# Own places in TensorE's order for scores, sums and values, by kind of segment, in a recurrent attention kernel with streamed weights

## The chip, the core and the metric

The kernel runs on one core of a Trainium2 chip. The metric is the device time of one launch in microseconds (us), the median over runs. Engines are named as in the profile: PE is TensorE's matmuls, PEld its weight loads, DVE is VectorE, ACT is ScalarE, POOL is GpSimd, SP is SyncE, which here only issues transfers (DMAs).

## The reference, cut to what matters

Two branches read the same layer-normed `x` (2048 rows of 1024) and are added to it: a dense branch with a GELU, and a recurrent attention.

```python
for s in range(n_seg):                       # 64 segments of 32 rows
    h = concatenate([mem, xs], axis=1)       # 8 memory rows and the segment's 32
    q, k, v = h @ Wq, h @ Wk, h @ Wv         # 1024 -> 32 heads of 128
    p = softmax(where(mask, q @ k.T * scale, -1e9))
    o = (p @ v) @ Wo                         # 4096 -> 1024
    mem = o[:, :M, :].copy()                 # the next segment's memory
    outs.append(o[:, M:, :])
```

A segment cannot begin before the one ahead of it has its 8 output memory rows. All four weight matrices are used in every segment, and they do not fit on the core together.

## The kernel before, in words

**Two stages.** The first (up to about 430 us) makes the dense branch for all rows and lays out, in DRAM, the transposed inputs and the residual rows of every segment. The second is the recurrence, 64 segments one after another, some 22 us each. The change touches the second alone.

**Weights.** Each of the four matrices is cut into 16 units of 128x2048 elements, 512 KB each. 46 of the 64 units stay on the core, 18 are `STREAMED` in each segment: 16 by a DMA from DRAM, 2 by a DVE copy out of PSUM (line 240). Six slots hold streamed units. When PE has used a streamed unit, `unit_done` (it is called after each unit) lets the slot go and starts the next transfer in the list on SP's queue (lines 251 and 253), so a transfer begins when PE releases a slot and has six streamed units of lead.

**The order within a segment.** PE's order is written out by hand. Six half passes of 8 units each come first, K0, Q0, K1, Q1, V0, V1 (the digit is the half of the heads, 16 heads each), and then 16 units of the output product, O. A unit of a half pass is four 128x512 products side by side, one per 32 columns of the array (line 705). `half_pass(w, u, left, at)` takes a dictionary `at` from a unit's number to pieces of work that stand in PE's order after that unit; the O loop has the same. These pieces are:

- `scores(u)`: 32 small products (lines 807 and 813) into the PSUM tile `mixed`, an exponential on ACT (819), two mask operations on DVE (826).
- `sums(u)`: 8 products that add up the exponentials (834, 840), then on ACT a logarithm and two exponentials (845, 848), then on DVE the two tiles of normalised weights, `pd_main` (855) and `pd_left` (859).
- `values(u, rs)`: for each of 4 columns of heads a main product with this segment's V (874) and a left product with V of the left rows (880). `rs` are the two row halves of the array; each half has its own PSUM bank and is copied out by ACT (half 0) or DVE (half 1), line 888.

**Left rows.** Only 24 of the 32 rows of a segment go with its own pass; the last 8 rows of the four segments of a group are done together, as extra products (`hL`, "left") on the same units. Which passes carry them depends on the place in the group, `i4 = s % 4`, so there are four kinds of segment. Kind 0 carries left products in K1 and V0, kind 1 in Q0 and in O (twice the length), kind 2 in Q1, kind 3 in K0 and V1. A unit with left products takes PE twice as long.

**The Q1 and V1 passes around the change.** The transposition of Q1 that `scores(1)` needs runs thus: `sums(0)` in the Q1 pass; on ACT the logarithm and exponentials of `sums(0)`, then the cast of Q1 (line 749, `b_oL`); on DVE `pd_main`, `pd_left`, and only then the transposition (763). Both engines work in the order of their instructions. PE meanwhile does the rest of Q1, the whole of V0, and the first unit of V1. In kind 0 the left rows of V0 are cast by DVE (753, tile `VL`) just ahead of `values(0)`. In kind 2 `keep_q(1)` copies queries into a part of `mixed` (line 240) between `scores(0)` and `sums(0)`. The results of `values(1)` are the inputs (`b_oL`) of O's units 8 to 15, those of `values(0)` (`d_oL`) of units 0 to 7. Three PSUM banks (`acc`) go round among the passes and the values.

Of the kernel before, what the change touches and what calls it, by code (L numbers as in the profile page):

```python
# [86 lines left out]
def kernel(  # L87
# [177 lines left out]
    def load_left_rows(g, eng=nc.sync):  # L265
        hr = hrp.tile([P, 256], BF16, name="hrL")
        eng.dma_start(out=hr[:, :], in_=hrL_d[g, :, 0:256])
        nxt["hL"] = hr.rearrange("p (k t) -> p k t", k=KT)
# [346 lines left out]
    with tc.tile_pool(name="late", bufs=1) as late, \  # L615
# [10 lines left out]
        def new_acc():  # L626
            bank = free_banks.popleft()
            ps = banks.tile([P, 512], F32, name="acc", tag=bank)
            bank_of[id(ps)] = bank, ps
            return ps  # L630

        def let_go(ps):
            free_banks.append(bank_of.pop(id(ps))[0])
# [47 lines left out]
        for s in range(NSEG):  # L681
            g, i4 = divmod(s, GRP)
# [96 lines left out]
            def q_left(u):  # L779

                if i4 >= 2 + u and more:
                    q = qS[:, i4 - 2 - u, :, :]
                else:
                    q = qL[u][:, :, NL * i4:NL * i4 + NL]
                nc.vector.tensor_copy(out=q_home[:, :, 0:NL], in_=q)

            def ends(t):

                return t.rearrange("p c (a b) -> p c a b", b=NL)[:, :, ::4, :]
# [9 lines left out]
            def scores(u, meanwhile=None):  # L799

                kT, qL_ends = st["kT", u], ends(q_home)
                sA = mixed[:, 0:160].rearrange("p (c q) -> p c q", q=40)
                sB = mixed[:, 160:224].rearrange("p (c q) -> p c q", q=16)
                for c in range(4):
                    for j in range(4):
                        q = slice(32 * j, 32 * j + 32)
                        nc.tensor.matmul(  # L807
                            sA[q, c, :], lhsT=kT[:, 4 * c + j, :], rhs=q_home[:, 4 * c + j, :],
                            start=(c == 0), stop=True, skip_group_check=True, tile_position=(0, 32 * j),
                        )  # L810
                    for j in range(4):
                        q = slice(32 * j, 32 * j + 32)
                        nc.tensor.matmul(
                            sB[q, c, :].rearrange("p (a b) -> p a b", b=NL), lhsT=kL[u][:, 4 * c + j, :],
                            rhs=qL_ends[:, 4 * c + j, :, :],
                            start=False, stop=True, skip_group_check=True, tile_position=(0, 32 * j),
                        )
                pr = pr_all[:, 0:224]
                nc.scalar.activation(out=pr, in_=mixed[:, 0:224], func=ACT.Exp, scale=INV_SQRT_DH)
                prA = pr[:, 0:160].rearrange("p (c q) -> p c q", q=40)  # L820
                prB = pr[:, 160:224].rearrange("p (c q) -> p c q", q=16)
                if meanwhile is not None:
                    meanwhile()
                for p, m in ((prA[:, :, NL:SEG], mask_order), (prB, mask_left[:, i4, :])):
                    n = m.shape[-1]
                    nc.vector.tensor_tensor(out=p, in0=p, in1=m[:, None, :].to_broadcast([P, 4, n]), op=ALU.min)
                st["pr", u] = prA, prB

            def sums(u):
                prA, prB = st["pr", u]  # L830
                dA = mixed[:, 0:160].rearrange("p (c q) -> p c q", q=40)
                for j in range(4):
                    q = slice(32 * j, 32 * j + 32)
                    nc.tensor.matmul(
                        dA[q, :, :], lhsT=bd[:, j:j + 1].to_broadcast([P, 32]), rhs=prA, start=True, stop=False,
                        skip_group_check=True, tile_position=(0, 32 * j),
                    )
                for j in range(4):
                    q = slice(32 * j, 32 * j + 32)
                    nc.tensor.matmul(  # L840
                        ends(dA[q, :, :]), lhsT=bd[:, j:j + 1].to_broadcast([P, 32]),
                        rhs=prB.rearrange("p c (a b) -> p c a b", b=NL),
                        start=False, stop=True, skip_group_check=True, tile_position=(0, 32 * j),
                    )
                nc.scalar.activation(out=mixed[:, 0:160], in_=mixed[:, 0:160], func=ACT.Ln)  # L845

                for b in (1, 0):
                    nc.scalar.activation(  # L848
                        out=mixed[:, 160 * b:160 * b + 160], in_=mixed[:, 0:160], func=ACT.Exp, scale=-1.0,
                        bias=off[:, b:b + 1],  # L850
                    )
                pdA = pd_main.rearrange("p (c b q) -> p c b q", c=4, b=2)
                pdB = pd_left.rearrange("p (c b a q) -> p c b a q", c=4, b=2, q=NL)
                dd = mixed[:, 0:320].rearrange("p (b c q) -> p b c q", b=2, q=40)
                nc.vector.tensor_tensor(  # L855
                    out=pdA.rearrange("p c b q -> p b c q"), in0=prA[:, None, :, :].to_broadcast([P, 2, 4, 40]),
                    in1=dd, op=ALU.mult,
                )
                nc.vector.tensor_tensor(
                    out=pdB.rearrange("p c b a q -> p b c a q"),  # L860
                    in0=prB.rearrange("p c (a q) -> p c a q", q=NL)[:, None, :, :, :].to_broadcast([P, 2, 4, 2, NL]),
                    in1=dd.rearrange("p b c (e q) -> p b c e q", q=NL)[:, :, :, ::4, :], op=ALU.mult,
                )
                st["pd", u] = pdA, pdB

            def values(u, rs):

                V, (pdA, pdB) = st["V", u], st["pd", u]
                av = {r: new_acc() for r in rs}
                oV = {r: av[r][:, 0:320].rearrange("p (c b q) -> p c b q", c=4, b=2) for r in rs}  # L870
                for c in range(4):
                    for r in rs:
                        q = slice(64 * r, 64 * r + 64)
                        nc.tensor.matmul(  # L874
                            oV[r][:, c, :, :], lhsT=V[q, c * P:(c + 1) * P], rhs=pdA[q, c, :, :],
                            start=(c == 0), stop=False, skip_group_check=True, tile_position=(64 * r, 0),
                        )
                    for r in rs:
                        q = slice(64 * r, 64 * r + 64)
                        nc.tensor.matmul(  # L880
                            oV[r].rearrange("p c b (e q) -> p c b e q", q=NL)[:, c, :, ::4, :],
                            lhsT=VL[u][q, c * P:(c + 1) * P], rhs=pdB[q, c, :, :, :],
                            start=False, stop=True, skip_group_check=True, tile_position=(64 * r, 0),
                        )
                for r in rs:
                    cp = nc.vector.tensor_copy if r else nc.scalar.copy
                    out = outs[u][:, 8 * r:8 * r + 8, NL * slot:NL * slot + 40]
                    cp(out=out.rearrange("p (b c) q -> p c b q", b=2), in_=oV[r])
                    let_go(av[r])
# [32 lines left out]
            at = {} if first else {1: [lambda: q_left(0)]}  # L922
# [7 lines left out]
            if left_q[0] and not first:  # L930
# [3 lines left out]
            rows_out(psK1, nat_home, nc.scalar.copy)  # L934
            at = {
                0: [lambda: scores(0, None if first else lambda: q_left(1)), lambda: nc.vector.transpose(out=nat_home, in_=nat_home)],
                6: [lambda: sums(0)],
            }
            if left_q[1] and not first:
                at[0].insert(1, lambda: keep_q(1))  # L940
# [14 lines left out]
                left_values(0, psVL)  # L955
            if i4 == 0 and more and not first:
                load_left_rows(g + 1, nc.scalar)
            at = {0: [lambda: scores(1)], 4: [lambda: sums(1)]}
            if left_v[1]:
                at.update({1: [lambda: values(0, (0,))], 3: [lambda: values(0, (1,))]})  # L960
            else:
                at[1] = [lambda: values(0, (0, 1))]

            def load_res():
                st["res"] = res_home
# [15 lines left out]
            if left_v[1]:  # L981
                at = {4: [lambda: values(1, (0,))], 6: [lambda: values(1, (1,))]}
            else:
                at = {5: [lambda: values(1, (0, 1))]}
            if left_v[1] and not first:
                at[9] = [lambda: left_values(1, psV1L)]
            at.setdefault(0, []).append(load_res)
# [42 lines left out]
            if final:  # L1030
                engines = [nc.sync, nc.scalar, nc.gpsimd]
                n = 0
# [57 lines left out]
```

The softmax here doesn't subtract the row's maximum and nothing guards it: scores larger than these inputs give would overflow.

## Time and profile before

| | us |
|---|---|
| median of three runs | 1876.3 |
| the runs | 1868.09, 1877.63, 1876.3 |
| span of the profiled execution, first to last instruction | 1866.2 |
| PE busy in it | 1726.3 |
| DVE, ACT, POOL busy | 904.3, 650.4, 257.7 |
| moved by DMA | 613.13 MB |

The profiled execution has no launch time of its own listed; its span is 1.9 us under the fastest run and 10.1 us under the median. In the profile the second stage begins near slice 9 or 10 of 40. A segment has about 1000 instructions on PE (a weight load and a product each), all in program order. A segment's time, taken from one copy of the new memory (DVE, line 289) to the next, has these means over segments 4 to 59, 14 of each kind: kind 0 22.53 us, kind 1 23.01, kind 2 20.89, kind 3 22.59; a group of four is 89.0 us, and 16 groups make the second stage.

When reading PE's rows, note that four products run side by side and each is shown 0.38 us long, while the next four start 0.21 us after them: idle time under some 0.17 us doesn't show as a gap, but shows as a longer step from one start to the next.

### The profile page before, as it was taken

The numbers are of one execution on the slowest core, as the hardware profiler recorded it, in microseconds if no ns is written. First come the engines' busy times: TensorE is split into PE (matmuls) and PEld (weight loads), VectorE is DVE, ScalarE is ACT, GpSimd is POOL, SyncE is SP. The second block draws the span as 40 slices with busy tenths as digits, with TensorE's granted clock in tenths as the row PEclk, the third lists the DMA queues.
The fourth block names the chain that finished last, engine by engine and source line by source line (L and its number), as shares of the span: only waits on it lengthen the run. The fifth ranks groups of instructions, "written<-read, shape, count | busy, mean of one in ns | idle before, by whom it ended". The sixth has DMA issues, their size and how long they took to land.

```text
span 1866.2 us, 72871 instructions
## 1 busy us (share of the span) xinstructions
PE 1726.3 (93%) x32208; PEld 938.2 (50%) x32228; DVE 904.3 (48%) x2190; ACT 650.4 (35%) x1384; POOL 257.7 (14%) x511
## 2 busy tenths in 40 slices
PE   7999999998999999988899999999999999999987
PEld 3444444444554555455555555555545454555544
DVE  6657483704444444444444444544444454544443
ACT  6434251602333333333333333333333333333333
POOL 0000000000442111111111211111111111111112
PEclk9999999999999999999999999999999999999999
DMA  9821211399999999999999999999999999999998
GB/s 337 268 57 47 53 45 53 127 364 334 400 382 393 384 397 379 367 364 368 368 377 380 378 392 394 399 390 384 382 384 390 387 381 378 389 402 384 395 372 318
DMA packets 219721, 613.13 MB, mean 329 GB/s; under 512 B 46507, under 2 KB 65755, under 8 KB 219404
## 3 DMA queue, kind: packets, MB, share of 16 engines
q1 hardware_dynamic: 199292, 589.38, 83.1%
q0 software_dynamic: 15872, 16.39, 2.7%
q8 instruction: 252, 4.13, 0.9%
q10 hardware_dynamic: 4240, 2.71, 0.5%
q14 instruction: 65, 0.53, 0.1%
HBM read 594.40 MB, written 29.23 MB: 334 GB/s over the span
## 4 chain that ended last, share of the span: by engine, by line
PE 65%; DMA 21%; DVE 5%; issue 4%; ACT 3%; POOL 1%; DVEq 0%; ACTq 0%; POOLq 0%; SPq 0%
PE acc L705 30%; PE ps L506 10%; DMA u<-Wc_K 10%; PE acc L902 9%; PE ps L555 8%; DMA u<-Wc_O 4%; DMA outL_d<-half_home 2%; DMA u<-Wc_Q 2%; PE ps L591 2%; ACT mixed L848 2%; PE acc L874 2%; DVE b_oL L763 1%; PE mixed L807 1%; DVE pd_main L855 1%; ACT mixed L845 1%
## 5 line engine op out<-in xcount | busy, mean ns | idle before, releaser
L705 PE MATMUL acc<-u,hr_home 128*32 128x512 bf16 x11520 | 784.3, 381 | 34.5 <-issue 11.8
L705 PEld LDWEIGHTS <-hr_home 128*32 128x32 bf16 x12288 | 353.4, 97 | 318.1 <-issue 64.5
L705 PE MATMUL acc<-u,hrL 128*32 128x512 bf16 x2880 | 261.7, 381 | 9.4 <-issue 5.7
L902 PE MATMUL acc<-u,d_oL 128*32 128x256 bf16 (+1 forms) x3552 | 179.7, 291 | 20.5 <-DMA u<-Wc_O 12.4
L506 PE MATMUL ps<-u 128*128 128x512 bf16 x896 | 196.1, 382 | 2.6 <-ACT u L390 2.6
L240 DVE TENSOR_SCALAR u<-kept 128x512 uint32<-128x512 uint32 x254 | 163.5, 686 | 29.2 <-PE acc L902 12.0
L555 PE MATMUL ps<-u 128*128 128x512 bf16 x657 | 146.2, 379 | 0.8
L902 PEld LDWEIGHTS <-b_oL 128*32 128x32 bf16 x3569 | 112.7, 99 | 67.8 <-issue 35.3
L506 PEld LDWEIGHTS <-u 128*128 128x128 bf16 x896 | 88.1, 98 | 109.3 <-issue 4.6
L902 PEld LDWEIGHTS <-d_oL 128*32 128x32 bf16 (+1 forms) x3552 | 104.0, 98 | 73.7 <-issue 32.6
L1052 POOL DMA_DIRECT2D out_dram<-hr_home x188 | 96.6, 515 | 308.8 <-DVE hr_home L1019 296.2
L855 DVE TENSOR_TENSOR pd_main<-half_home,mixed 128x320 bf16<-128x320 bf16 x128 | 62.5, 488 | 157.5 <-ACT mixed L848 155.7
L705 PEld LDWEIGHTS <-hrL 128*32 128x32 bf16 x3072 | 92.0, 96 | 61.6 <-issue 24.9
L763 DVE STREAM_TRANSPOSE b_oL<-b_oL 128x512 bf16<-128x512 bf16 x128 | 90.7, 708 | 62.5 <-ACT b_oL L749 62.5
L902 PE MATMUL acc<-u,b_oL 128*32 128x256 bf16 (+1 forms) x1618 | 107.0, 292 | 14.9 <-DMA u<-Wc_O 10.5
L902 PE MATMUL acc<-W_O,b_oL 128*32 128x256 bf16 (+1 forms) x1776 | 109.4, 291 | 4.7 <-issue 4.5
L262 POOL DMA_DIRECT2D hr_home<-hr_d x58 | 32.4, 558 | 585.1 <-PE acc L705 566.4
L749 ACT CAST kT<-acc 128x512 bf16<-128x512 f32 x64 | 37.5, 586 | 216.9 <-PE acc L705 216.9
L555 PEld LDWEIGHTS <-u 128*128 128x128 bf16 x672 | 65.3, 98 | 77.4 <-DVE g_u L522 0.4
L749 ACT CAST b_oL<-acc 128x512 bf16<-128x512 f32 x128 | 75.2, 587 | 82.1 <-PE acc L705 81.3
L1004 ACT CAST d_oL<-acc 128x256 bf16<-128x256 f32 (+1 forms) x63 | 26.9, 427 | 209.3 <-PE acc L902 209.3
L514 ACT ACTIVATE g_xb<-ps,b1col 128x512 bf16<-128x512 f32 x112 | 76.8, 686 | 61.0 <-PE ps L506 59.8
(123 smaller groups left out, 1968.3 us busy)
## 6 DMA issues: line engine op xcount, KB each, us to landing
u<-Wc_K SPq DMA_DIRECT2D x320, 512.0 KB
u<-Wc_V SPq DMA_DIRECT2D x256, 512.0 KB
u<-Wc_O SPq DMA_DIRECT2D x256, 512.0 KB
u<-Wc_Q SPq DMA_DIRECT2D x128, 512.0 KB
u<-Wc_O SPq DMA_DIRECT2D x64, 320.0 KB
hr_home<-hr_d POOLq DMA_DIRECT2D x58, 128.0 KB, 5.5
u<-in_B_w_dram SPq DMA_DIRECT2D x14, 512.0 KB
u<-in_A_Wq_dram SPq DMA_DIRECT2D x14, 512.0 KB
```

What stands on the lines that cost most here:

```text
L240: nc.vector.tensor_single_scalar(out=out, in_=in_, scalar=0, op=ALU.bitwise_or)
L506: nc.tensor.matmul(ps[:, :].rearrange("p (s t) -> p s t", t=SEG), lhsT=w1_sb[fb // 14 * 8 + kt][:, (fb % 14) * P:(fb % 14 + 1) * P], rhs=x ...
L514: nc.scalar.activation(out=xb[:, :], in_=ps[:, :], func=ACT.Identity, bias=b1col[:, fb:fb + 1], scale=1.0)
L555: nc.tensor.matmul(ps[:, :], lhsT=gts[fc // 4][:, fc % 4, t * P:(t + 1) * P], rhs=w2_sb[fc // 2][:, fc % 2, cs], start=(fc == 0), stop=(fc ...
L591: nc.tensor.matmul(pss[2 * t + nb][:, :], lhsT=gts[fc // 4][:, fc % 4, t * P:(t + 1) * P], rhs=w2_sb[fc // 2][:, fc % 2, nb * 512:nb * 512 ...
L705: nc.tensor.matmul(o, lhsT=lhs[:, i, :], rhs=m, start=(i == seq[0]), stop=(i == seq[-1]), tile_position=(0, 32 * j),)
L749: cp(out=out, in_=ps.rearrange("p (h e) -> p h e", e=32))
L763: nc.vector.transpose(out=home, in_=home)
L848: nc.scalar.activation(out=mixed[:, 160 * b:160 * b + 160], in_=mixed[:, 0:160], func=ACT.Exp, scale=-1.0, bias=off[:, b:b + 1],)
L855: nc.vector.tensor_tensor(out=pdA.rearrange("p c b q -> p b c q"), in0=prA[:, None, :, :].to_broadcast([P, 2, 4, 40]), in1=dd, op=ALU.mult,)
L902: nc.tensor.matmul(acc[r:r + n // 8, c:c + wide], lhsT=lhs[:, 4 * (i % 4) + 2 * u + k, :], rhs=w_t[:, c0 + c:c0 + c + wide], start=(unit = ...
L1052: nc.gpsimd.dma_start(out=out_flat[rows, 256 * j:256 * j + 256], in_=res[32 * j:32 * j + NX, :])
```

## The change

In the Q1 pass `sums(0)` stands after unit 7 in kind 2, after unit 6 as before in the others. In the V1 pass and in O the places are these (the unit after which a piece stands):

| kind | scores(1) | values(0) | sums(1) | values(1), in O |
|---|---|---|---|---|
| 0 before | 0 | 1 | 4 | 5 |
| 0 after | 0 | 2 | 4 | 5 |
| 1 before | 0 | 1 | 4 | 5 |
| 1 after | 2 | 3 | 6 | 5 |
| 2 before | 0 | 1 | 4 | 5 |
| 2 after | 1 | 3 | 5 | 6 |
| 3 before | 0 | 1 and 3 | 4 | 4 and 6 |
| 3 after | 1 | 2 and 4 | 5 | 4 and 6 |

The very first segment takes kind 3's places in V1; the last group's segment of kind 3, which has no left rows in V1, takes 1, 3, 5 and 5. In `values` all main products of the four columns now stand ahead of all left products. No instruction is added or taken away on any engine: the orders of ACT, DVE, POOL and SP are the same as before, and PE has the same 64458 instructions in another order.

```diff
@@ values
                             start=(c == 0), stop=False, skip_group_check=True, tile_position=(64 * r, 0),
                         )
+                for c in range(4):
                     for r in rs:
                         q = slice(64 * r, 64 * r + 64)
                         nc.tensor.matmul(
@@ the Q1 pass
-                6: [lambda: sums(0)],
+                7 if i4 == 2 else 6: [lambda: sums(0)],
@@ the V1 pass
-            at = {0: [lambda: scores(1)], 4: [lambda: sums(1)]}
             if left_v[1]:
-                at.update({1: [lambda: values(0, (0,))], 3: [lambda: values(0, (1,))]})
+                at = {
+                    1: [lambda: scores(1)], 2: [lambda: values(0, (0,))], 4: [lambda: values(0, (1,))],
+                    5: [lambda: sums(1)],
+                }
+            elif i4 == 0:
+                at = {0: [lambda: scores(1)], 2: [lambda: values(0, (0, 1))], 4: [lambda: sums(1)]}
             else:
-                at[1] = [lambda: values(0, (0, 1))]
+                n = 2 if i4 == 1 else 1
+                at = {n: [lambda: scores(1)], 3: [lambda: values(0, (0, 1))], n + 4: [lambda: sums(1)]}
@@ O
             else:
-                at = {5: [lambda: values(1, (0, 1))]}
+                at = {6 if i4 == 2 else 5: [lambda: values(1, (0, 1))]}
```

## The prediction

> **What bounds the kernel now.** I read the page's busy shares, slices and chain first.
>
> ```profile
> PE 1726.3 (93%) x32208; PEld 938.2 (50%) x32228; DVE 904.3 (48%) x2190; ACT 650.4 (35%) x1384; POOL 257.7 (14%) x511
> ...
> PEclk9999999999999999999999999999999999999999
> DMA  9821211399999999999999999999999999999998
> GB/s 337 268 57 47 53 45 53 127 364 334 400 382 393 384 397 379 367 364 368 368 377 380 378 392 394 399 390 384 382 384 390 387 381 378 389 402 384 395 372 318
> ...
> PE 65%; DMA 21%; DVE 5%; issue 4%; ACT 3%; POOL 1%; DVEq 0%; ACTq 0%; POOLq 0%; SPq 0%
> ```
>
> From slice 10 on, PE and the DMA engines are both nearly full: two limits lie close together. The rate ranges from 364 to 402 GB/s in full slices, so most slices are below what the transfers can do. The windows of one whole group (kinds 0, 1, 2, 3) say which kind has which limit.
>
> ```profile
> 979.50:1002.60 23.10, 20.34 (x512) 13.13 (x504) 10.38 (x25) 7.74 (x18) 2.60 (x5) 1.00 1.00 375
> 1002.60:1026.20 23.60, 21.96 (x417) 11.17 (x417) 10.42 (x27) 7.47 (x17) 3.16 (x6) 1.00 1.00 385
> 1026.20:1048.30 22.10, 18.74 (x476) 10.53 (x468) 10.63 (x28) 7.36 (x17) 5.21 (x10) 1.00 1.01 373
> 1048.30:1069.90 21.60, 20.76 (x512) 12.39 (x508) 10.16 (x26) 7.76 (x18) 2.64 (x5) 1.00 1.00 380
> ```
>
> PE (second number) is idle 0.8 to 3.4 us; kind 2, with the least left work, is idle longest. PE's own waits over 500 to 1850 us:
>
> ```profile
> PE acc L902 <- DMA u<-Wc_O: 22.4, 51, 1.3
> ...
> PE mixed L807 <- DVE b_oL L763: 10.9, 39, 0.4
> PE acc L705 <- DMA u<-Wc_K: 9.9, 24, 1.2
> ...
> PE mixed L834 <- DVE mixed L240: 3.1, 6, 0.8
> ```
>
> The first is O waiting for streamed units; sorted by segment, 40 of the 51 waits, 1.27 us per segment, are in kind 2. The second is `scores(1)` waiting for transposed queries: 0.35 us per segment in kind 1, 0.19 in kind 2, 0.16 in kind 3, none in kind 0. The timeline of a kind 1 segment shows why:
>
> ```profile
> 1012.99 0.59 ACT L749 CAST b_oL<-acc 128x512 bf16<-128x512 f32 x1
> ...
> 1013.09 0.49 DVE L855 TENSOR_TENSOR pd_main<-half_home,mixed 128x320 bf16<-128x320 bf16 x1 [1.83 <-ACT mixed L848]
> ...
> 1013.50 0.28 DVE L859 TENSOR_TENSOR pd_left<-half_home,mixed 128x128 bf16<-128x128 bf16 x1
> ...
> 1013.70 0.70 DVE L763 STREAM_TRANSPOSE b_oL<-b_oL 128x512 bf16<-128x512 bf16 x1
> ...
> 1014.45 0.20 PE L807 MATMUL mixed<-b_oL,d_oL 128*32 128x40 bf16 x4 [0.41 <-DVE b_oL L763]
> ```
>
> The transposition stands behind the two products of `sums(0)` on DVE and ends at 1014.40; PE had finished V1's unit 0 and stood idle for 0.41 us although seven units of V1 needed nothing of it. In kind 0 `values(0)` hits another thing:
>
> ```profile
> 992.52 0.69 DVE L753 CAST VL<-acc 128x512 bf16<-128x512 f32 x1 [1.19 <-PE acc L705]
> ```
>
> ```profile
> 993.08 0.38 PE L874 MATMUL acc<-pd_main,v 64*128 64x80 bf16 x2
> 993.27 0.20 PE L880 MATMUL acc<-pd_left,VL 64*128 64x32 bf16 x2
> ```
>
> The cast of the left V ends at 993.21, the first main pair has started at 993.08, and the first left pair, which otherwise follows 0.04 us later, starts at 993.27. That shows in no wait row, as gaps under 0.15 us are not counted.
>
> **What the Trainium skill says.** "TensorE: Matmul & The Clock Gate", section on the step-by-step of a matmul: products stay in program order, only weight loads are pulled ahead. The trace agrees: one waiting score product held V1 for 0.41 us. The same page, section "Wait — 56ns, not 53.3ns?", puts the least distance between two small products at about 25 ns; here a left product's successor comes 26 to 36 ns later, a main product's 35. "DMA: Bandwidth & Descriptors", Specifications, gives a fabric ceiling of 435 GB/s and some 358 per core from HBM; here full stretches run at 400 to 410 (kind 2, 6 to 20 us into the segment), so the measurement stands. Its section on the anatomy of one DMA has a fixed part of about 2 us, mostly the receipt; in this trace PE starts on awaited O units about 1.6 us or more after their last byte.
>
> **The change part by part.** Steps are start to start on PE, means over the 14 groups of segments 4 to 59.
>
> Kind 1, scores from after unit 0 to after unit 2: the step from V1's unit 0 to the scores is 0.75 us, against 0.22 for a free unit. Two units of 0.215 us now lie ahead: 0.43 us of the excess 0.53 are covered. Saved: 0.43.
>
> Kind 3, scores after unit 1, which carries left products (0.43 us): the left half of unit 0 takes 0.58 against 0.28 free. Saved: 0.30, all of it.
>
> Kind 0, values after unit 2 and mains first: the block takes 0.54 against 0.34 in kind 1. Starting 0.22 later, with eight mains (0.14 us) ahead of the first left, it finds `VL` cast. Saved: 0.20.
>
> Kind 2, three moves. `sums(0)` behind unit 7: before, the step ahead of it is 0.53 against 0.22 (in part the wait for line 240), 0.31 us that go. But the sums start about 0.43 - 0.22 = 0.21 us later in absolute time (unit 7 has left products), and with them the logarithm, the cast, the transposition; scores after unit 1 have 0.21 us more cover. The queries come about 0.2 later, PE arrives there at nearly the old time: the scores wait 0.4 instead of 0.2 to 0.36. Sum 0 (bounds 0.15 saved, 0.2 lost). `values(1)` behind O's unit 6: its copies (ACT 0.43, DVE 0.49, and about 0.13 for two hand-overs) had units 6 and 7 (0.43 us) for cover and now have unit 7; O's unit 8 may wait 0.2 to 0.4. Kind 2's waits for units 5, 7, 10 and 13 of O cover that; without them it would cost 0.2 to 0.4 per group.
>
> Later sums: 0.43 us of V1 later in kind 1, less the 0.43 saved; nearly the same in kind 3. `pd_left` ends 0.9 us (kind 3) to 1.5 us (kind 1) ahead of `values(1)` in the medians, so nothing waits. Mains first by itself: 8 distances of 35 and 26 to 36 ns in either order; 0, bounds 0.03 us for each of nine calls per group. Queues: ACT, DVE, POOL and SP keep their orders; streamed units 1 of V1 (kinds 1, 2, 3), 6 of V1 (kind 1) and 7 of Q1 (kind 2) are released ahead of scores or sums, so SP's issues come earlier, none later by the order itself.
>
> Sum on PE: 0.43 + 0.30 + 0.20 + 0 = 0.93 us per group, 14.9 us over 16 groups.
>
> How much reaches the end is the choice that decides. A group moves 34.2 MB; at 405 GB/s that is 84.4 us, against 89.0 measured, so 4.6 us of slack in transfers are there for 0.93. And it lies where it is wanted: the rate falls to about 340 GB/s in O of kind 0, 290 to 350 in O of kind 3 and 340 in the first 5 us of kind 2, each right after a saving, as PE releases slots too slowly there. But PE also waits for transfers in K0 of kinds 0, 1, 3 (0.18 to 0.24 us each) and in kind 2's O. A saving ahead of such a wait is kept only as far as the transfer is issued earlier too. I take 0.7 kept: 0.65 us per group, 10.4 us, 0.56% of the span. The same off the median gives 1866. All kept would be 1861, a third 1871.
>
> **The rivals.** *Transfers take it back.* DMA is shown full everywhere, and every PE gain ahead of kind 2 could turn into a longer wait in kind 2's O. For it: the share of 1.00 in all windows. Against it: rates far under 405 next to the savings. A third to a half kept gives 1869 to 1872, within 0.5%.
>
> *Kind 2 becomes the loser.* The late `sums(0)` delays the cast of Q1, which frees the bank that V1 starts in (0.05 to 0.15 us), the scores (0.2) and O's unit 8 (0.4): 0.75 us per group, 12 us. It decides once PE no longer waits 1.27 us for streamed units in kind 2's O, and the others' gain is mostly taken back: 1876 + 12 - 3 = 1885. For it: three pieces of kind 2 move later at once. Against it: those waits total 18 us in this very kind.
>
> *The change doesn't do what it says*: the queries could come later by as much as the scores move. In kinds 1 and 3 nothing ahead of the transposition moves (sums(0) stays after unit 6), so this is excluded there; it is what I expect in kind 2.
>
> **How the numbers follow.** A run-to-run change of about 0.5% (9.4 us; the three runs lie 9.5 apart) can just be told from none. Forecast with 0.6 or more kept: chance 0.55, 1857 to 1867.5. Transfers take it: 0.31, 1868 to 1877. Kind 2 loses: 0.11, 1878 to 1890. The rest, 0.03, is more than all of the sum, from transfers issued earlier. The forecast's case reaches slightly into the 0.5% band, so faster 0.53, same 0.36, slower 0.11. The range, 1856 to 1880, leaves out most of the third case and the far gain.
>
> **What would show it.** Right: the wait of L807 for L763 falls from 11.9 us in the whole span to under 5, what is left being kind 2's; the step into kind 1's scores falls to some 0.3; kind 0's values block takes 0.35; L834 no longer waits for L240; a group takes 88.4 us. The wait for `Wc_O` grows in kind 2 by 1 to 5 us in total. Wrong: that wait grows by over 8 us with the group at 89 (first rival), or rows of L902 waiting for line 889 (once 888) in kind 2 with longer segments (second).

## The result, and the profile after

| | before | after |
|---|---|---|
| median, 12 runs each, compared on one chip | 1873.04 us | 1876.01 us |
| the runs | 1868.09 to 1878.35 | 1865.52 to 1882.07 |
| after / before | | 1.000, 95% interval 0.998 to 1.002 |
| span of the profiled execution | 1866.2 us | 1876.9 us (its launch took 1878.6 us) |
| a group of four segments in it (segments 4 to 59) | 89.0 us | 89.7 us |

The change makes no difference that can be measured. Forecast were 1866 us and, with a chance of 0.53, a gain of over 0.5%; the range of 1856 to 1880 held the time.

From the page of the kernel after come the busy shares, the slices and the chain:

```profile
PE 1721.6 (92%) x32208; PEld 940.1 (50%) x32228; DVE 905.6 (48%) x2190; ACT 650.7 (35%) x1384; POOL 256.9 (14%) x511
...
DMA  9821211499999999999999999999999999999998
GB/s 338 264 57 47 54 49 49 146 352 339 386 398 384 381 395 364 381 375 357 357 368 370 367 390 387 391 393 378 392 377 371 381 367 390 393 397 388 390 391 315
...
PE 45%; DMA 18%; issue 4%; DVE 2%; ACT 1%; POOL 0%; DVEq 0%; POOLq 0%; ACTq 0%
```

Nothing here explains the result: the same work, the same rate of transfer, "issue" at 4% in both chains (the shares of this chain add up to 70%, so it covers only a part of the span). The windows of one group of after, in the order kind 1, 2, 3, 0 (the numbers of a line are the length, then busy time and instructions of PE, PEld, DVE, ACT and POOL, the granted clock, the DMA share, GB/s):

```profile
1099.10:1121.60 22.50, 21.71 (x425) 11.56 (x417) 10.51 (x27) 7.48 (x17) 3.13 (x6) 1.00 1.01 395
1121.60:1142.00 20.40, 18.18 (x476) 10.41 (x468) 10.63 (x27) 7.36 (x17) 5.19 (x10) 1.00 1.03 400
1142.00:1164.60 22.60, 20.68 (x508) 12.60 (x508) 10.07 (x25) 7.81 (x18) 2.61 (x5) 1.00 0.98 373
1164.60:1187.50 22.90, 20.61 (x512) 12.13 (x504) 10.48 (x26) 7.82 (x18) 2.59 (x5) 1.00 1.01 395
```

PE, the second number, is idle 0.8 to 2.3 us per segment (0.8 to 3.4 in the group shown of before; this group's 88.4 us are a little under the mean). What it waits for did change. PE's waits over 500 to 1850 us, after (each line: engine, tile, line of the kernel, what ended the wait, total us, times, longest):

```profile
PE acc L903 <- issue: 24.9, 33, 2.0
PE acc L705 <- issue: 24.9, 30, 1.8
PE acc L903 <- DMA u<-Wc_O: 20.4, 50, 1.7
PE acc L705 <- DMA u<-Wc_K: 8.2, 14, 2.2
PE acc L874 <- issue: 6.6, 5, 1.9
PE mixed L807 <- issue: 5.5, 7, 1.3
...
PE mixed L807 <- DVE b_oL L763: 2.8, 12, 0.4
```

And the rows of the same view of before that the prediction left out between those it showed:

```profile
PE acc L705 <- issue: 18.6, 32, 1.4
PE acc L902 <- issue: 13.8, 24, 1.6
...
PE acc L880 <- issue: 7.0, 8, 2.2
```

Line 705 is the half passes, 902 or 903 the products of O, 807 the scores. The scores' wait for transposed queries fell from 10.9 to 2.8 us. The waits for streamed units of O did not grow (22.4 before). "Issue", a wait that nothing in the profile's semaphores explains, grew in its two largest rows from 32.4 to 49.8 us.

Both sides can be seen in one place. The timeline of a kind 1 segment of after, at the scores:

```profile
1016.62 0.24 PE L834 MATMUL mixed<-half_home,small_consts 128*32 128x160 bf16 x1 [0.84 <-issue]
...
1016.73 2.75 PE L705 MATMUL acc<-u,hr_home 128*32 128x512 bf16 x45
...
1018.71 0.70 DVE L763 STREAM_TRANSPOSE b_oL<-b_oL 128x512 bf16<-128x512 bf16 x1
...
1019.47 0.20 PE L807 MATMUL mixed<-b_oL,d_oL 128*32 128x40 bf16 x4
```

The transposition ends at 1019.41, PE is busy with V0 and V1 up to the scores and takes them without a wait; before, it stood idle there for 0.41 us. But 2.9 us earlier, at `sums(0)`, it stood idle for 0.84 us, and the profile shows nothing that it waited for. In kind 0, PE's timeline at `values(0)`:

```profile
1090.38 0.32 PE L874 MATMUL acc<-pd_main,v 64*128 64x80 bf16 x8
1090.53 0.26 PE L881 MATMUL acc<-pd_left,VL 64*128 64x32 bf16 x8
1090.72 0.61 PE L705 MATMUL acc<-u,hr_home 128*32 128x512 bf16 x7
1091.89 0.39 PE L705 MATMUL acc<-u,hr_home 128*32 128x512 bf16 x1 [0.56 <-issue]
```

The left products follow the mains without a gap, as forecast, and 1.4 us later PE stands still between two products of the same pass for 0.56 us.

### The profile page after: what moved, and what is told of

It reads as the page before. It is cut to its first block, busy times and chain, and to the rows that moved or that the text cites. A ratio compares the mean times of both kernels' runs of the same rounds, so it can differ in the third digit from the quotient of the medians.

```text
span 1876.9 us, 72886 instructions
## 1 busy us (share of the span) xinstructions
PE 1721.6 (92%) x32208; PEld 940.1 (50%) x32228; DVE 905.6 (48%) x2190; ACT 650.7 (35%) x1384; POOL 256.9 (14%) x511
## 4 chain that ended last, share of the span: by engine, by line
PE 45%; DMA 18%; issue 4%; DVE 2%; ACT 1%; POOL 0%; DVEq 0%; POOLq 0%; ACTq 0%
PE acc L705 32%; PE acc L903 9%; DMA u<-Wc_K 7%; DMA u<-Wc_O 7%; DMA u<-Wc_V 2%; DMA outL_d<-half_home 2%; PE acc L874 1%; PE mixed L807 1%; DMA u<-Wc_Q 1%; PE mixed L813 1%; DVE u L240 1%; PE acc L881 1%; PE mixed L834 0%; ACT mixed L848 0%; DVE b_oL L763 0%
## 5 line engine op out<-in xcount | busy, mean ns | idle before, releaser
L705 PEld LDWEIGHTS <-hr_home 128*32 128x32 bf16 x12288 | 347.2, 96 | 327.0 <-issue 77.7
L705 PEld LDWEIGHTS <-hrL 128*32 128x32 bf16 x3072 | 89.7, 96 | 63.0 <-issue 24.4
L514 ACT ACTIVATE g_xb<-ps,b1col 128x512 bf16<-128x512 f32 x112 | 76.8, 686 | 60.9 <-PE ps L506 59.8
```

What stands on the lines that cost most here:

```text
L514: nc.scalar.activation(out=xb[:, :], in_=ps[:, :], func=ACT.Identity, bias=b1col[:, fb:fb + 1], scale=1.0)
L705: nc.tensor.matmul(o, lhsT=lhs[:, i, :], rhs=m, start=(i == seq[0]), stop=(i == seq[-1]), tile_position=(0, 32 * j),)
```

## The experiments

Three theories were set against each other. **I** (instruction supply): PE lacks instructions in these gaps, and the saved waits come back as such gaps. **T** (transfers): PE reaches the streamed units earlier and waits there, the prediction's first rival. **K**: kind 2's three moves lose what the others gain, its second rival. Two more, R and S, are named in the expectations that use them.

For every run, all of PE's idle gaps of over 0.15 us in the second stage (from the first copy of the memory to the last) were added up from the trace, by what ended them. All runs are in one table, in us:

```
                             issue  DVE, ACT  DMA    sum    time of launch, median
before                        47.9    21.3    35.2   104.6   1873.0
before again                  55.3    22.1    36.3   113.7   1875.1 (one run)
after                         74.2    11.6    34.2   120.0   1876.0
after again                   74.4    11.1    33.9   119.4   1882.2 (one run)
after without kind 2's moves  74.1    12.8    31.4   118.3   1875.6
before with kinds 1 and 3     61.3    14.5    34.4   110.5   1872.1
half O, before                14.1    24.5    47.0    85.6   1832.8
half O, after                 12.7    16.7    55.5    84.9   1833.5
light, before                 25.8    25.1    29.9    81.6   1817.0
light, after                  34.8    16.2    24.5    75.5   1808.4
half and light, before         2.2    33.6    40.5    76.3   1810.3
half and light, after          2.4    24.9    33.6    60.9   1790.5
folded, before                11.0    37.5    37.9    86.4   1844.4
folded, after                 19.9    25.7    41.0    87.0   1840.6
```

The gaps are those of one profiled execution, the time in the last column is a median of launches. The two need not go together: launches of one kernel lie up to 19 us apart (27 of before took 1864 to 1884 us), and in the first six rows the length of the profiled second stage less its sum of gaps is always 1269 to 1276 us. So a larger sum in these rows says that this execution was longer, not that the kernel is; the division among the three columns is what tells kernels apart. The ratios below are to runs of before made beside each kernel (medians 1874.7, 1871.7 and 1873.6 us).

### The two kernels once more

No edit; each is run and profiled once more.

> A second profile of the kernel before, to tell what of a profile belongs to the kernel and what to the run. The first one has 47.9 us of PE idle in front of instructions that waited for nothing that the profile shows (issue), 21.6 for DVE, 38.7 for DMA. Theory I (instruction supply takes the gain: PE's idle 'issue' time, each piece of which ends about 1.4 us after a 16 KB packet of the instruction queue, is larger in the changed order, 74.2 us): here again 40 to 55 us of it. Theory R (that difference is only the run): anything from 45 to 75.

> A second profile of the changed kernel. Theory I: again 65 to 85 us of 'issue' idle time, some 25 more than the kernel before, while the waits for DVE stay near 12. Theory R: about the same as the second profile of before, within 10 us. Theory T (transfers take it back): the waits for DMA together exceed those of before by 8 us or more.

Measured: 1875.09 us for before, 1882.17 for after. PE's waits over 500 to 1850, of before again and then of after again:

```profile
PE acc L902 <- issue: 21.6, 28, 1.9
PE acc L705 <- issue: 19.7, 32, 1.7
...
PE mixed L807 <- DVE b_oL L763: 10.6, 39, 0.4
```

```profile
PE acc L903 <- issue: 28.9, 33, 3.1
PE acc L705 <- issue: 24.7, 35, 2.1
...
PE mixed L807 <- DVE b_oL L763: 3.2, 14, 0.4
```

So the exchange belongs to the kernels and not to one execution: waits for DVE and ACT fall from 21 to 22 us to 11 to 12, issue waits rise from 48 to 55 us to 74. How much they rise is less sure, since both profiled executions of after were longer (spans of 1876.9 and 1880.5 us against 1866.2 and 1873.4). The 55.3 us of before are just over the 40 to 55 expected.

### Kind 2 left as it was

```diff
-                7 if i4 == 2 else 6: [lambda: sums(0)],
+                6: [lambda: sums(0)],
...
-                n = 2 if i4 == 1 else 1
-                at = {n: [lambda: scores(1)], 3: [lambda: values(0, (0, 1))], n + 4: [lambda: sums(1)]}
+                n = 2 if i4 == 1 else 0 if i4 == 2 else 1
+                at = {n: [lambda: scores(1)], 1 if i4 == 2 else 3: [lambda: values(0, (0, 1))], n + 4: [lambda: sums(1)]}
...
-                at = {6 if i4 == 2 else 5: [lambda: values(1, (0, 1))]}
+                at = {5: [lambda: values(1, (0, 1))]}
```

> The change without its three moves in kind 2. Theory K (kind 2 loses what the others gain; its segments are 0.45 us longer in the profile after): 8 to 10 us faster than before, ratio 0.995. Theory I or T (the saved waits come back as other waits wherever they are saved): within 0.2% of before.

Measured: 1875.64 us, 1.0006 of before (0.9986 to 1.0027). Taking the suspected loss away gains nothing; at most 0.14% is left open. Kind 2's moves are not what hides the gain, and theory K falls.

### Only the moves in kinds 1 and 3

The V1 pass gets the new places in these two kinds, all else is before's.

```diff
-            at = {0: [lambda: scores(1)], 4: [lambda: sums(1)]}
...
+                at = {
+                    1: [lambda: scores(1)], 2: [lambda: values(0, (0,))], 4: [lambda: values(0, (1,))],
+                    5: [lambda: sums(1)],
+                }
...
+                n = 2 if i4 == 1 else 0 if i4 == 2 else 1
+                at = {n: [lambda: scores(1)], 1 if i4 == 2 else 3: [lambda: values(0, (0, 1))], n + 4: [lambda: sums(1)]}
```

> Only the later scores, values and sums of the V1 pass in kinds 1 and 3; values keep main and left products by turns, kinds 0 and 2 as before. By my sum this alone saves 0.73 us per group on PE, 11.7 us. Theory K: faster by 6 to 10 us. Theories I and T: within 0.2% of before, with the wait of the scores for the transposition down by 7 us in the profile and as much more idle time for instructions (I) or for DMA (T).

Measured: 1872.09 us, 0.998 (0.9957 to 1.0006). These two moves were to bring 0.73 of the 0.93 us per group, 11.7 us. DVE and ACT waits fell by about 7 us, issue waits stand between those of before and after. A gain of up to 0.4% is not excluded; the 0.62% that 11.7 us would be is.

### What an issue wait is

Before the next runs the gaps were set against the DMA records. The page lists a queue whose kind is "instruction":

```profile
q8 instruction: 252, 4.13, 0.9%
```

That is 252 packets of 16 KB. PE has 64458 instructions, 255.8 per packet. The Trainium skill, "Runtime: NRT & Kernel Launch", section "Instruction fetch mechanics", says what this is: each engine's instructions come in blocks of 16 KiB, 256 instructions, through a queue of the sequencer's own; it adds that crossing into a new block is mostly hidden. The first half agrees with the 252 packets. The second holds here for two crossings of three: of 229 in the second stage of before, 77 had a gap, and these gaps add up to 47.9 us. They can be told from others by their place. If each gap is put at its place in PE's order (counted in products, each of which has one weight load), the gaps stand at equal distances, like the teeth of a comb.

```
                                                      before   after   half O, after
issue gaps in the second stage                          77       93       22
on a comb of one tooth in 127.7 to 127.8 products,
  within one product                                    72       89       20
products still ahead of PE as a block's packet starts   54       53       70    (median, all blocks)
us from the previous block's first product to that      3.14     3.23     2.81  (median, all blocks)
the same, for the blocks that PE waited for             3.5      3.6      3.4   (median)
us from that to the block's first product, in gaps      2.39     2.38     2.47  (median)
us that a block lasts when the next one stalls          5.94     5.94     5.85  (median)
```

By chance one or two of 93 gaps would lie that near a tooth. The packets say the same: 76 of the 77 gaps of before and all 93 of after end 1.2 to 1.65 us after the end of an instruction packet (median 1.42), but only 11 of 144 and 7 of 106 of PE's other gaps do. At random moments the last packet's end lies a median 3.0 us back, mostly 0.3 to 6.1. So issue gaps are PE standing at the end of a block while the next is not there.

A gap opens when PE gets through a block sooner than the next one comes. For the blocks that PE waited for, the packet started 3.5 us after the previous block's first product, and PE went on 2.4 us after that, together the 5.9 us. That is no least time for a block: all blocks of the stage last 6.0 us on average, and 38% of them under 5.6 us. How long does PE need for one without waits? A pass has 4 products per 0.215 us, so 128 last 6.9 us. O of kinds 0, 2 and 3 has 8 products of half the width per 0.22 us, so 128 last 3.5 us, and scores and values are denser still. A block with such a stretch in it is soon through, and the gap comes at its end, often in the pass behind. PE's timeline in O of a kind 0 segment of after:

```profile
907.12 1.48 PE L903 MATMUL acc<-u,d_oL 128*32 128x256 bf16 x48
908.53 0.32 PE L874 MATMUL acc<-pd_main,v 64*128 64x80 bf16 x8
908.68 0.26 PE L881 MATMUL acc<-pd_left,VL 64*128 64x32 bf16 x8
908.87 0.29 PE L903 MATMUL acc<-u,d_oL 128*32 128x256 bf16 x4
911.20 0.83 PE L903 MATMUL acc<-u,d_oL 128*32 128x256 bf16 x12 [2.04 <-issue]
```

PE stops in the middle of a unit, after 4 of its 8 products, for 2.04 us; the unit's data had been used by the four before.

This would also say what a saved wait is worth, though it is argued and not shown alone: if the next block comes no sooner for it, a dependency wait inside a block that ends in a gap only fills time in which PE would have stood there anyway. In before 5.4 of the 11.9 us of the scores' waits lie in such blocks, and 2.5 more run into a wait for a streamed unit within the next 130 products.

### Half as many instructions in O

In kinds 0, 2 and 3 each unit of O is computed by 4 products of 512 columns, as in a half pass, instead of 8 of 256. The two heads of a unit then land in different rows and their partial sums are not added: that sum is left out.

```diff
-                (w, i, u), n = unit, 512 if left_o else 256
+                (w, i, u), n = unit, 512
...
-                        r, c0 = n // 8 * jq, DM * k + n * jq
+                        wr = 64 if left_o else 32
+                        r, c0 = (64 * jq if left_o else 64 * k + 32 * jq), DM * k + n * jq
```

> The order of before, with half the instructions in O for kinds 0, 2 and 3: instead of eight 256-column products a unit has four of 512 columns, the two heads of a unit in separate column groups, so the same number of columns passes the array in the same time. Left out: the sum of the two heads' partial results, so memory and output are not the reference's. Transfers, the order, the waits on ACT and DVE stay; PE has 5,900 fewer instructions, 92 a segment. Theory I (PE is short of instructions in O): the idle time marked issue falls from 48 to 55 us to under 30, in O of kinds 0, 2 and 3 from 15 to 23 us to under 6, and the kernel is 8 to 25 us faster than before. Theory T (transfers alone bound the stage there): waits for streamed units grow instead, within 5 us of before.

> The same halving of O's instructions, with the same part left out, in the changed order. Theory I: here the savings of the changed order are kept: issue time under 35 us instead of 74, and 6 to 12 us faster than the halved kernel in the order of before. Theory T: equal to it within 4 us, waits for DMA 8 us or more above its.

Measured: 1832.82 us, 0.979 (0.9735 to 0.9843), in the order of before; 1833.51, 0.978 (0.9739 to 0.9828), in that of after. PE's waits over 500 to 1800, half O in the order of before, then of after:

```profile
PE acc L903 <- DMA u<-Wc_O: 23.9, 53, 1.8
PE acc L705 <- DMA u<-Wc_K: 18.9, 40, 1.7
PE mixed L807 <- DVE b_oL L763: 11.3, 41, 0.4
```

```profile
PE acc L904 <- DMA u<-Wc_O: 31.6, 68, 1.7
PE acc L705 <- DMA u<-Wc_K: 15.4, 38, 1.1
PE acc L705 <- DMA u<-Wc_V: 6.6, 16, 0.9
...
PE mixed L807 <- DVE b_oL L763: 3.0, 14, 0.3
```

Issue waits fell to 13 to 14 us and the time by 39 us, more than the 8 to 25 expected: the supply of instructions did hold the kernel. Not all of the 39 us are waits that the table counts. The second stage without its gaps is 13 us shorter too (1260 to 1262 us, against 1269 to 1276), some 5 to 8 us of it in O's own steps; whether that was waits too short to be counted or the narrower products themselves, the runs don't say.

The order of after is no faster here as far as can be told (-1.1 ± 10.4 us, worked out from the spread of four runs each, so a gain of 6 to 11 us is not excluded). In the traces the 7.8 us of DVE and ACT waits that it saves come back as 8.5 us of waits for streamed units, as theory T has it, with both kernels at 393 GB/s in that window.

### Lighter transfers

Four of the sixteen units transferred in each segment bring only 512 of their 2048 columns, and their products are taken with those (left out: the products with the other three quarters of these four units; the columns that did come are used in their place).

```diff
+LITE = [("K", 5, 1), ("V", 4, 0), ("V", 3, 1), ("O", 2, 1)]
...
+        elif n >= 2 * STREAMED and unit in LITE:
+            nc.sync.dma_start(out=t[:, 0:512], in_=copies[unit][:, 0:512])
```

> The order of before with lighter transfers: from segment 2 on, four of the 16 transferred units (one each of K1, V0, V1, O) bring 512 of their 2048 columns, and PE multiplies these 512 four times over in place of the rest. 1.57 MB less per segment, 19% of the streamed weights; the products with the other columns of these units are left out (replaced), PE's instructions, columns and order stay. Transfers and instruction fetches then have room. All theories: the waits for DMA fall from 38 us to under 10, issue falls too; 40 to 80 us faster than before.

> The changed order with the same lighter transfers and the same products replaced. If the saving on PE is real and only transfers or instruction fetches over the full DMA engines take it back (theories I and T): 8 to 15 us faster than the light kernel in the order of before. If the saving was never there (theory S, the dependency waits were hiding other work): equal within 4 us.

Measured: 1817.03 us (0.9685, 0.9635 to 0.9735) and 1808.37 (0.9647, 0.9585 to 0.9709). The order of after is 8.7 us faster by the medians of four runs each, but the interval of the difference, worked out from the runs' spread, is -8.9 ± 14 us: no gain lies in it as well as the whole one, so this pair decides nothing about theory S. The waits for DMA were to fall under 10 us and are still 29.9 and 24.5: a miss. Issue waits fell to 26 to 35 us, though no instruction was taken away. With the load at 323 to 326 GB/s a block's packet starts 2.3 us after the previous block's first product (medians), against 3.1 to 3.4 in the first six kernels of the table, while the packet takes 0.96 us, not 1.01. The load is not the whole of it: in the half kernels, at 393 GB/s, the packet starts after 2.8 us.

### Both at once

The edits of the two pairs together.

> The order of before, with O in half as many instructions and four of the sixteen transferred units bringing 512 of 2048 columns (left out: the sum of the two halves of O's partial sums, and three quarters of those four units; their products are taken with the columns that did come). Neither the instruction queue nor the streamed units should hold PE here: PE's issue waits under 20 us and its waits for streamed units under 20 us in 500 to 1800. Each relief alone gave 1833 and 1817; together 1780 to 1805 if they add in good part. The wait of the scores for the transposed queries stays at 11 to 13 us. Only beside the next kernel does it tell theories apart.

> The same two reliefs in the order of after (left out: the same as in the kernel beside it). If instruction supply and transfers together are what takes the change's gain (theories I and T): nothing is left to take it, and this is faster than the order of before by 9 to 15 us (0.6 to 0.93 us per group), the wait of the scores for the queries at 3 to 4 us against 11 to 13. If the moves lose on PE itself as much as they save (theory K or another of that sort): within 4 us of the order of before here too.

Measured: 1810.26 us (1802.82 to 1812.61, six runs), 0.9645 of before (0.9613 to 0.9678), and 1790.52 us (1785.36 to 1796.72, six), 0.9547 (0.9515 to 0.9579). The two sets of runs don't touch; the order of after is faster by 18.4 ± 5.1 us, 1.0%. PE's waits over 500 to 1800, order of before, then of after:

```profile
PE acc L713 <- DMA u<-Wc_K: 24.1, 41, 1.6
PE acc L913 <- DMA u<-Wc_O: 16.4, 27, 1.7
...
PE mixed L816 <- DVE b_oL L772: 12.8, 46, 0.4
```

```profile
PE acc L713 <- DMA u<-Wc_K: 18.1, 38, 2.1
PE acc L914 <- DMA u<-Wc_O: 15.8, 26, 1.8
...
PE mixed L816 <- DVE b_oL L772: 3.6, 16, 0.4
```

This pair shows that the saving on PE is real. With issue waits nearly gone (2.2 and 2.4 us) and the load at 327 GB/s the moves bring 1.15 ± 0.32 us per group, the 0.93 of the sum or more, which refutes S as well as K. In the traces the waits for DVE and ACT fall by 8.7 us and those for DMA by 6.9. In the first pair this gain is taken back, in part at least by instructions that were not there, as the comb shows. How much belongs to transfers is not settled, since the pair with their relief alone decided nothing.

Two expectations were missed. The first kernel took 1810 us where 1780 to 1805 was expected, and the streamed units still held PE for 40.5 and 33.6 us in the stage where under 20 was expected. That is what is left of both kernels' gaps, with the waits for DVE and ACT (33.6 of the 76.3 us in the order of before).

### A complete kernel with half of O's instructions

The partial sums of the two heads stay apart in PSUM, 32 rows each, and are added on the way out. The new memory was brought into place by an identity matrix, and the part for the residual rows was read straight; both now go through a folding matrix (two identities side by side, added) that sums the two. It costs one more DVE copy and four small products in each segment of kinds 0, 2 and 3. The matrix takes the place of 64 resident columns of a weight unit, so 16 KB more are transferred in each segment (not shown in the cut edit). The second run is the same edit on the order of after.

```diff
+                nc.vector.tensor_tensor(
+                    out=half_home[:, PART_COLS:768], in0=ident[:, 0:64], in1=ident[:, 64:128], op=ALU.add,
+                )
...
+                if not left_o:
+                    nc.vector.tensor_copy(
+                        out=o_sb[:, 8:16, :], in_=psX[:, 256:512].rearrange("p (h e) -> p h e", e=32)
+                    )
...
-                put_mem(o_sb, nxt["hT"], mixed[:, 224:288], 4 // nw)
+                put_mem(o_sb, nxt["hT"], mixed[:, 224:288], 2, None if left_o else fold[:, :, NX:SEG])
+                if not left_o:
+                    psR = new_acc()
+                    for j in range(4):
+                        nc.tensor.matmul(
+                            psR[32 * j:32 * j + 32, 0:256].rearrange("p (h e) -> p h e", e=32), lhsT=fold[:, j // 2, :],
+                            rhs=o_sb[:, 8 * (j % 2):8 * (j % 2) + 8, :],
+                            start=True, stop=True, tile_position=(0, 32 * j),
+                        )
+                    let_go(psX)
+                    psX = psR
```

> A complete kernel in the order of before: O in half as many instructions, the partial sums of the two heads kept apart in PSUM (32 rows each) and added by the matrix that brings the sums back into place (a folding matrix in place of the identity, four more small products per segment, one more copy on DVE). Theory I: PE's issue waits in the second stage fall from 48 to 55 us to under 20, and of the 39 us that the half kernel gained, 20 to 35 stay: 1840 to 1855, 1 to 2% faster than before. If issue waits only stood where PE would have waited anyway: within 0.5% of before, or slower by the added work (about 0.5 us per segment, 30 us).

> The same folded O in the order of after, a complete kernel. If transfers take what the moves save once instructions no longer do (as the two half kernels showed, equal within 0.5%): within 5 us of the folded kernel in the order of before. If the moves' gain is kept here: 8 to 12 us faster than it.

Measured: 1844.38 us, 0.983 (0.9795 to 0.9863), and 1840.64, 0.982 (0.9779 to 0.9865). Both are as expected, and both beat the two kernels of the case by about 1.7%. No difference between them is shown (-1.6 ± 7.9 us; a gain of 8 to 9 us for the order of after is just not excluded). Waits over 500 to 1800 of the folded kernel in the order of before, then of after:

```profile
PE acc L907 <- DMA u<-Wc_O: 26.9, 62, 1.1
PE mixed L809 <- DVE b_oL L765: 11.0, 41, 0.4
PE mixed L287 <- DVE d_oL L1014: 10.9, 45, 0.2
```

```profile
PE acc L908 <- DMA u<-Wc_O: 31.7, 72, 2.4
PE mixed L287 <- DVE d_oL L1020: 10.6, 44, 0.2
PE acc L707 <- issue: 7.7, 16, 1.0
...
PE mixed L809 <- DVE b_oL L765: 3.0, 14, 0.2
```

The new wait at line 287, 0.2 us per segment of these kinds for the second copy, is the largest that folding adds. Here again what the moves save on DVE (11.8 us with ACT) comes back in the trace, 8.9 us as issue and 3.1 as transfers.

## Why the prediction was right and wrong

The savings on PE were forecast well, and what becomes of them was not. That the range of 1856 to 1880 us holds the time is luck as far as the mechanism goes: it was wide enough to hold a kernel that doesn't change at all.

**Kind 1's scores: right.** Saved 0.43 was forecast. The step from V1's unit 0 fell from 0.75 to 0.23 us, the step into the scores is 0.34. Of the excess of 0.53, 0.14 is left. In the half and light pair, where hardly an issue gap is mixed in, the step into the scores falls from 0.82 to 0.39: 0.43.

**Kind 3's scores: right.** The left half of V1's unit 0 takes 0.22 instead of 0.58, that of unit 1, now ahead of the scores, 0.28: 0.30 saved, as worked out (0.60 to 0.22 in the half and light pair).

**Kind 0's values: right in the median.** The block takes 0.34 us in the median, 0.40 in the mean, where 0.35 was forecast and 0.54 stood (median 0.51); the rest of the mean is issue gaps. Mains first by itself changed nothing, as forecast: in kind 1 the block takes 0.34 in the median in either order. The 25 ns that the prediction names as the least distance between two small products fit these blocks' pairs alone: the scores' products, four side by side, start a median of 4 ns apart.

**Kind 2 at nothing: right within its bounds.** That the kernel takes 1876.0 us with these moves and 1875.6 without doesn't show it, since gains don't show in this time either. The steps do: the step into `sums(0)` fell from 0.53 to 0.36 us (0.31 was to go; the wait of line 834 for line 240 fell from 3.1 to 1.2 us, not to none), the step into the scores stayed (0.58 and 0.55), and V1 begins 0.20 us later (0.42 for 0.22 from V0's last unit), which the prediction has in its second rival, at 0.05 to 0.15, and not in the sum.

**The sum of 0.93 us per group: right.** With both reliefs the same moves brought 1.15 ± 0.32.

**How much reaches the end: wrong, and this is the step that failed.** "I take 0.7 kept" was worked out from transfers alone: 84.4 us for a group's bytes, 4.6 us of slack. The other limit was put at nothing without a reason, although it stood in the second and third row of the view that the prediction quotes, between the lines shown: issue, which over the stage, with 47.9 us, is more than twice all waits for DVE and ACT. A group has some 14 blocks of 256 instructions; of the 229 blocks of the stage PE stood still for 77 before and for 93 after. In place of 0.7, nothing that can be measured was kept in these two kernels (the interval allows some 4 us of 14.9).

**"The wait for `Wc_O` grows by 1 to 5 us": wrong.** It fell from 22.4 to 20.4. PE hardly came to O earlier: from a segment's start to its first product of O it took 59.8 us per group before and 59.9 after (60.1 and 60.3 in the second profiles), where most of 0.93 less was the sum; issue gaps on the way had grown.

**The first rival, transfers take it back:** nearer in size (1869 to 1872), not in the cause. Its sign, this wait growing by over 8 us with the group at 89, was not seen in the kernel after (89.7, against 89.0 and 89.5 in the two profiles of before, and the wait fell). It was seen in the half kernels, once instructions were there in time. **The second rival** fell with the third experiment and with the half and light pair, which has kind 2's moves in it. **That the change doesn't do what it says** is excluded by 10.9 to 2.8 us.

What stays open: issue waits grew by 19 to 26 us in the first pair, more than the 10 us by which dependency waits shrank. A part of this belongs to the executions, which were longer for after; in the light and the folded pairs issue grew by 9.0 and 8.9 us where dependency waits shrank by 8.9 and 11.8. And that a block's fetch starts late because it stands behind the streamed units is argued, not shown alone: its start moved from 3.1 to 2.3 us after the previous block's first product when the load fell from some 380 to 325 GB/s, which fits the Trainium skill, "DMA: Bandwidth & Descriptors", section "Queues, rings and completion order", which says that each DMA engine goes round the queues that have work, a packet at a time; but the waits around it had changed too, and in the half kernels it moved to 2.8 us with the load at 393 GB/s.

## What to carry to other kernels

A wait that is removed counts only up to the next thing that was not going to be ready anyway, so list every row of the bounding engine's waits with its total, "issue" among them, before saying how much of a saving is kept. Where an engine stands still in the middle of a run of like instructions with no semaphore to wait for, set the gaps against the instruction queue's packets and against the count of instructions: gaps that stand only at the ends of blocks of 256 instructions, each soon after such a packet, were a limit of supply here. Then fewer, larger instructions in the dense stretch can be worth more than a better order, here 1.7% against nothing measurable. The better order on top of them still brought nothing that could be measured; it did so only with lighter transfers as well.

## What the runs showed of the hardware that was not expected

- PE can be short of instructions. Under 380 to 393 GB/s of transfers, 77 and 93 of the 229 blocks of 256 instructions in the stage were awaited; 76 of the 77 gaps and all 93 ended 1.2 to 1.65 us after the end of an instruction packet. The fetch of a block began with a median of 53 to 54 products of the block before it still ahead.
- 512-wide products on 32 columns take about the same time per unit (0.216 us) as 256-wide ones at twice the number (0.219), so halving the number cost PE nothing and gained 2.1% with the sum of the heads left out, 1.7% with it.
- A saving on PE can be there and not show: with the relief of instructions alone no difference between the two orders was shown (-1.1 ± 10.4 us), with that of transfers alone it was -8.9 ± 14, with both -18.4 ± 5.1.
